# Seventeen zero products in place of thirty-six at the head of a fused attention and feed-forward kernel, with a new order

## The chip, the cores and the metric

The kernel runs on one core of a Trainium2 chip. The metric is the device time of one execution in microseconds (us). The time of the kernel before is the median of three runs. A profile of one more execution was taken by the hardware profiler.

## The reference

A sequence of 2048 rows of 576 values (bf16) passes one block: layer norm, attention with 32 heads of 18 values in four segments of 512 rows, with a memory carried from segment to segment, output projection and residual, then layer norm and a two-layer feed-forward part of width 4608 with gelu, and a second residual.

```python
q, k, v = x @ wq, x @ wk, x @ wv          # split in H=32 heads, N=4 segments
phi = lambda t: jnp.where(t > 0, t + 1.0, jnp.exp(t))
for s in range(N):
    p = _softmax(einsum('bhqd,bhkd->bhqk', qs, ks) * scale + mask)
    a_dot = einsum('bhqk,bhkd->bhqd', p, vs)
    a_mem = einsum(phi(qs), M) / (einsum(phi(qs), z) + 1e-06)
    o = g * a_mem + (1.0 - g) * a_dot      # g = sigmoid(beta), one for each head
    M, z = M + einsum(phi(ks), vs), z + sum(phi(ks))
...
h = x + o_all @ wo                         # attention was given layernorm(x)
h2 = h + (gelu(layernorm(h) @ w1 + b1) @ w2 + b2)
```

## The kernel before, in words

The rows are handled in eight chunks (c) of 256, each of two tiles (t) of 128 rows. A chunk passes projection (`project`), attention (`attend`, with `memory_of` for the memory part), output projection and second layer norm (`output`), `first_layer` (width 4608 in 36 blocks of 128) and `second_layer`. While one chunk is in attention, another is in its feed-forward part.

**Five queues, one list.** The kernel first defines all its steps as operations (`op`, `dma`): each has a name, an engine, the function that issues its instructions, and, for some, a second engine that can do the same work. The operations have running numbers. A list of numbers, `ORDER`, written out by hand into the file, then issues them; what one engine gets, it works off in that order. PE is TensorE (matrix products and transposes), DVE is VectorE, ACT is ScalarE, POOL is GpSimd; SP issues all DMAs.

- `PLACE` gives the PSUM bank of each accumulator. Four banks (0 to 3) are fixed; four more (4 to 7) serve either as single banks or, all four together, as the target of one group of score products (L623). A bank can be written again when its last reader is done.
- `FLIP` holds the operations that go to their second engine.
- `WHOLE` concerns the depth of 576 = 4 x 128 + 64. The last 64 rows of two products can be multiplied side by side in the two halves of the array (`tail`, lines 443 and 750), ahead of their four full products (line 350). For the pairs in `WHOLE`, each product has a full-height last product instead (line 354), with zeros or copies of rows in the other half.

**The head.** At the start PE has nothing to do until the first tile of x is loaded, normalized (statistics L365 and L366, subtraction L379, a copy of the last 64 columns L396, all on DVE), transposed by PE (L409, with an identity that POOL builds) and copied to SBUF (`PTcx`, L412 on DVE or L413 on ACT). Then the first projections run, which also need the weights: `wqkvr` (last 144 columns of wq or wk), `wqkv` (first 432 columns, or all of wv) and `wqkvt` (the last 64 rows, in parts). For the first two tiles the projection is cut into ch 4 (last columns of q and k), ch 1 (k), ch 0 (q), ch 5 and ch 3 (v). To fill the time, PE multiplies zeros:

```python
    for z in range(ZEROS):
        w = warm[min(z, 3)]
        n = 512 if z < 4 else Q
        op(("zeros", z), "PE", lambda w=w, n=n: nc.tensor.matmul(out=bank(w)[:, 0:n], lhsT=pq[:, 0, :], rhs=flat[:, 0:n], start=True, stop=True),
           ["pq"], [w])
```

That is four products of 512 columns and the rest of 256 (Q), on the buffer `pq` that DVE cleared (L333 in the profile). No result of theirs is read. In the order before, 19 stand ahead of the transpose of tile 0 and 17 between it and the transpose of tile 1; then come ch 4 of tiles 0 and 1, ch 1 of both, the transposes of k of tile 0 (`PTk`, L531), ch 0 of both, and so on. Meanwhile ACT, DVE and POOL clear paddings (L259, L292, L308), and `g_exp` (L336, ACT) takes the exponential of beta for the gates.

**DMAs.** SP has in the order before: x tile 0, `wqkvr` of wq, x tile 1, a tail of wk, x tile 2, `wqkvr` of wk, a tail of wq, a tail of wk (54 KB), the main part of wk, beta, the main part of wq, a tail of wv, x tile 3, wv, b1, and then wo, w1 and w2 in parts among the x tiles that follow. Some transposes are DMAs too (`Tx`, `Tk`, `Tq`, `Th`).

**Later steps that are named.** In `first_layer` a bias addition (`F1e`) moves each accumulator to SBUF, on DVE (L771) or, if flipped, ACT (L769); ACT then applies gelu (L792). In attention ACT takes the exponential of a group of 16 score products (L627), POOL masks (L631), PE multiplies with v (L639). `second_layer` is L852. `res` (L686) adds the residual; `MZ` (L561) sums the memory.

Of the kernel before, what the change touches and what calls it, by code (L numbers as in the profile page):

```python
# [16 lines left out]
def kernel(  # L17
# [43 lines left out]
    ZEROS = 36  # L61
# [4 lines left out]
    def sbuf(name, shape, dt=BF16):  # L66
# [29 lines left out]
    }  # L96
    FLIP = {
# [7 lines left out]
    }  # L105
    WHOLE = {
        265, 398, 408, 418, 425, 488, 489, 562, 871, 872, 1104, 1105, 1520, 2160, 2161,
# [221 lines left out]
    warm = [Tok(b) for b in range(4)]  # L329
    for z in range(ZEROS):  # L330
        w = warm[min(z, 3)]
# [547 lines left out]
    for c in range(NCH):  # L879
# [193 lines left out]
```

## Time and profile before

| What | us |
|---|---|
| timed runs | 454.94, 456.51, 457.49 |
| median | 456.51 |
| profiled execution, its own time | 454.46 |
| its span, first to last instruction | 452.4 |
| PE busy | 446.7 |
| ACT busy | 336.1 |
| DVE busy | 267.0 |
| POOL busy | 230.1 |

The span is the profiled part; 2.1 us of the execution lie outside of it. Rows of a timeline have start, length, engine, line of the kernel, instruction, and the tiles written and read; neighbouring instructions of one kind are merged (x19), and brackets tell the idle time ahead of the row and what ended it. Matrix products overlap, so that the length of a single one is more than the distance between two starts.

### The profile page before, as it was taken

The page shows a single profiled execution, that of the slowest core. Times are in us where ns is not written, and L with a number is a line of the kernel's source. Part 1 is how long each engine was busy: PE and PEld are TensorE (multiplying, and loading weights), DVE is VectorE, ACT ScalarE, POOL GpSimd, SP SyncE. Part 2 cuts the span into 40 slices and gives each one's busy share as a digit, 9 for nine tenths or more (in the row PEclk, how much of TensorE's full clock was granted, in tenths as well). Part 3 has the DMA queues.
Part 4 walks back from the last instruction along what each step waited for, and adds up shares of the span by engine and source line. Part 5 has one row for each costly group of instructions (what it writes and reads, how often), then busy time and mean ns, then how long its engine had stood idle before and what let it go on. Part 6 is the DMA issues. An engine that isn't in the chain of part 4 may idle for free.

```text
span 452.4 us, 14531 instructions
## 1 busy us (share of the span) xinstructions
PE 446.7 (99%) x6109; PEld 334.5 (74%) x6109; DVE 267.0 (59%) x612; ACT 336.1 (74%) x327; POOL 230.1 (51%) x414
## 2 busy tenths in 40 slices
PE   8999999999999999999999999999999999999997
PEld 5656887676776777776777667777777888888886
DVE  6989999776868667766665967554432441122311
ACT  7999899988889878879889778797954652634430
POOL 5789775788784678562756775654103302000000
PEclk9999999999999999999999999999999999999999
DMA  6998599945699638698855956785664575655211
GB/s 183 233 251 259 143 207 277 218 103 136 143 183 237 178 101 223 155 173 199 179 159 128 213 143 153 217 232 167 202 185 126 158 195 159 168 178 165 95 54 52
DMA packets 114353, 78.40 MB, mean 173 GB/s; under 512 B 48832, under 2 KB 112240, under 8 KB 114288
## 3 DMA queue, kind: packets, MB, share of 16 engines
q1 hardware_dynamic: 114288, 77.48, 67.4%
q8 instruction: 47, 0.77, 0.7%
q14 instruction: 18, 0.15, 0.1%
HBM read 60.09 MB, written 7.08 MB: 148 GB/s over the span
## 4 chain that ended last, share of the span: by engine, by line
PE 98%; DVE 1%; ACT 0%; issue 0%
PE bank L350 30%; PE bank L852 25%; PE st L350 10%; PE st L852 7%; PE st L623 6%; PE bank L639 5%; PE bank L750 3%; PE bank L683 3%; PE bank L354 2%; PE bank L333 2%; PE st L683 1%; PE bank L593 1%; PE st L750 1%; PE bank L531 1%; PE bank L561 1%; PE bank L443 1%
## 5 line engine op out<-in xcount | busy, mean ns | idle before, releaser
L627 ACT ACTIVATE pt<-st 128x2048 bf16<-128x2048 f32 x80 | 150.1, 1876 | 40.2 <-PE st L623 34.5
L852 PEld LDWEIGHTS <-hT 128*128 128x128 bf16 x1188 | 112.3, 98 | 26.8 <-issue 0.2
L852 PE MATMUL bank<-w_sb,hT 128*128 128x288 bf16 x900 | 127.4, 286 | 0.0
L350 PEld LDWEIGHTS <-w1g 128*128 128x128 bf16 x944 | 86.4, 98 | 19.1 <-issue 7.1
L631 POOL TENSOR_SCALAR_AFFINE_SELECT pt<-pt 128x512 bf16<-128x512 bf16 x128 | 80.6, 645 | 36.7 <-ACT pt L627 36.3
L350 PE MATMUL bank<-xn2T,w1g 128*128 128x256 bf16 (+1 forms) x776 | 96.5, 269 | 0.0
L771 DVE TENSOR_TENSOR hT<-bank,b1T 128x512 bf16<-128x512 f32 x78 | 52.6, 684 | 57.9 <-PE bank L350 56.6
L792 ACT ACTIVATE hT<-hT 128x1536 bf16<-128x1536 bf16 (+4 forms) x25 | 65.9, 2658 | 1.7 <-DVE hT L771 1.4
L769 ACT ACTIVATE hT<-bank,b1T 128x256 bf16<-128x256 f32 x66 | 27.4, 473 | 18.2 <-PE bank L350 18.0
L350 PE MATMUL bank<-wqkv,xT 128*128 128x432 bf16 (+2 forms) x188 | 39.5, 340 | 0.0
L350 PEld LDWEIGHTS <-xT 128*128 128x128 bf16 x264 | 23.7, 98 | 18.5 <-issue 2.4
L852 PE MATMUL st<-w_sb,hT 128*128 128x288 bf16 (+1 forms) x288 | 35.5, 271 | 0.0
L654 DVE STREAM_TRANSPOSE bank<-bank 128x512 f32<-128x512 f32 x32 | 23.2, 725 | 18.4 <-PE bank L639 11.9
L769 ACT ACTIVATE hT<-st,b1T 128x256 bf16<-128x256 f32 x28 | 11.7, 471 | 29.8 <-PE st L350 28.8
L588 POOL TENSOR_TENSOR pq<-ek,pq 128x512 bf16<-128x512 bf16 x24 | 27.8, 1159 | 10.8 <-DVE ek L587 10.4
L623 PE MATMUL st<-QT,KT 32*128 32x128 bf16 x1280 | 32.2, 217 | 0.8 <-DVE hT L771 0.8
L623 PEld LDWEIGHTS <-KT 32*128 32x128 bf16 x1280 | 18.6, 92 | 16.9 <-issue 14.0
L858 DVE TENSOR_TENSOR ot<-bank,hc 128x288 bf16<-128x288 f32 x25 | 11.3, 451 | 28.2 <-PE bank L852 23.5
L586 POOL TENSOR_SCALAR pq<-QT 128x512 bf16<-128x512 bf16 x24 | 14.8, 615 | 19.9 <-PE bank L593 12.0
L639 PE MATMUL bank<-pt,v_aug 128*19 128x128 bf16 x1280 | 24.0, 220 | 0.0
L691 POOL TENSOR_TENSOR h_t<-h_t,b_bc 128x576 f32<-128x576 f32 x16 | 20.4, 1278 | 6.2 <-ACT xn L714 4.3
L771 DVE TENSOR_TENSOR hT<-st,b1T 128x512 bf16<-128x512 f32 x19 | 12.7, 681 | 17.0 <-PE st L350 17.0
(160 smaller groups left out, 663.4 us busy)
## 6 DMA issues: line engine op xcount, KB each, us to landing
w1g<-in_B_w_dram SPq DMA_DIRECT2D x57, 512.0 KB, 4.1
w_sb<-in_B_w_dram SPq DMA_DIRECT2D x12, 432.0 KB, 5.2
wqkv<-in_B_w_dram SPq DMA_DIRECT2D x10, 512.0 KB, 4.4
hd<-h_t SPq DMA_DIRECT2D x16, 288.0 KB, 3.4
hc<-hd SPq DMA_DIRECT2D x32, 144.0 KB, 2.5
w1g<-in_B_w_dram SPq DMA_DIRECT2D x114, 32.0 KB, 3.5
x_b<-in_A_x_dram SPq DMA_DIRECT2D x18, 144.0 KB, 3.5
hT<-in_B_w_dram SPq DMA_DIRECT2D x5, 512.0 KB, 5.0
```

The costliest lines, as they stand in the source:

```text
L350: nc.tensor.matmul(out=acc, lhsT=lhsT_of(slice(0, P), k), rhs=rhs_of(slice(0, P), k), start=start and k == 0, stop=False, skip_group_check ...
L588: op(("m_add", n), "POOL", lambda: nc.gpsimd.tensor_tensor(out=pq[:], in0=e_g, in1=pq[:], op=ALU.add), ["ek"], ["pq"])
L623: nc.tensor.matmul(out=st4[:, i, n * P:(n + 1) * P], lhsT=KTs[(2 * s0 + kt) % NK][rows, g, :], rhs=QTs[(2 * c + qt) % NQ][rows, g, :], sta ...
L627: op(("exp", v), "ACT", lambda pt=pt: nc.scalar.activation(out=pt[:], in_=open_four("scores")[:], func=ACT.Exp, scale=scale), [st], [("pt" ...
L631: op(("mask", v), "POOL", lambda n=n, pt=pt: nc.gpsimd.affine_select(out=pt[:, :, n * P:(n + 1) * P], in_=pt[:, :, n * P:(n + 1) * P], pat ...
L639: nc.tensor.matmul(out=bank(ox)[32 * i:32 * i + E, (g % 4) * P:(g % 4) * P + P], lhsT=v_augs[(2 * s0 + kt) % NV][:, G * i + g, :], rhs=pt[ ...
L654: op(("f_T", n), "DVE", lambda: nc.vector.transpose(out=bank(ox), in_=bank(ox)), [], [ox])
L691: op(("hb", t), "POOL", lambda: nc.gpsimd.tensor_tensor(out=h_t[:], in0=h_t[:], in1=b2_bc[:], op=ALU.add), ["b2"], hk)
L769: nc.scalar.activation(out=dst[:, j, :], in_=acc()[:, j, :], func=ACT.Identity, bias=b1T[:, j0 + j:j0 + j + 1], scale=1.0)
L771: op(name, "DVE", lambda: nc.vector.tensor_tensor(out=dst, in0=acc(), in1=bias, op=ALU.add), [tok, "b1T"], keys, alt=("ACT", by_act), afte ...
L792: op(("gelu", c, f0, f), "ACT", lambda: nc.scalar.activation(out=hT[:, f0:f, :], in_=hT[:, f0:f, :], func=ACT.Gelu_apprx_tanh), [], [("hT" ...
L852: nc.tensor.matmul(out=bank(b)[:, 0:w], lhsT=hT[:, q, tl * P:(tl + 1) * P], rhs=w2_sb[:, q, hs], start=(q == 0), stop=(q == NF - 1))
```

## The change

`ZEROS` is 17 instead of 36. `PLACE`, `FLIP`, `WHOLE` and `ORDER` hold other values throughout. Numbers of operations behind the zeros are lower by 19, so the lists must be read by names; what follows was read that way.

- Zero products: 11 ahead of the transpose of tile 0, 4 ahead of that of tile 1, 2 behind it. Then ch 4 of tiles 0 and 1, ch 1 of both, `PTk` of tile 0, ch 0 of both, as before; the transpose of tile 2 (`PTx`) comes two places earlier than before, ahead of ch 5.
- SP: x tile 0, `wqkvr` of wk, x tile 1, x tile 2, beta, a tail of wq, `wqkvr` of wq, a tail of wk, the main part of wk, the 54 KB tail of wk, the main part of wq, x tile 3, a tail of wv, wv, a tail of wv, x tiles 4 and 5, two chunks of w1 (512 KB each), a part of wo, b1, the DMA transpose of tile 3.
- ACT: ten clears, with `g_exp` in eighth place among them, ahead of the copy of xT of tile 0 (before: eleven clears, `g_exp` behind the copies of both tiles). The copy of xT of tile 1 goes from ACT to DVE.
- DVE: ahead of the first statistics stand the clears of `pq` and of `MZacc`, the constant `mhalf`, one padding, and one clear of weights (before: eight clears).
- POOL: six clears, then the identity (before: the identity first).
- Banks: ch 4 and ch 1 of a tile share a bank (3 for tile 0, 4 for tile 1); before they had one each.
- `WHOLE`: 13 pairs instead of 15. Other bank for 278 of 363 accumulators. `FLIP` has 130 entries instead of 134.

```diff
-    ZEROS = 36
+    ZEROS = 17
...
     PLACE = {
-        0: 0, 1: 1, 2: 2, 3: 3, 4: 1, 5: 4, 6: 5, 7: 5, 8: 3, 9: 1, 10: 2, 11: 5, 12: 3, 13: 4, 14: 4, 15: 6, 16: 4,
...
+        0: 0, 1: 1, 2: 2, 3: 3, 4: 2, 5: 2, 6: 5, 7: 3, 8: 3, 9: 0, 10: 1, 11: 2, 12: 3, 13: 4, 14: 6, 15: 4, 16: 4,
...
     FLIP = {
-        15, 24, 26, 28, 33, 39, 44, 48, 49, 50, 51, 57, 60, 61, 66, 151, 153, 155, 157, 161, 173, 175, 177, 179, 181,
...
+        15, 28, 29, 31, 32, 33, 34, 35, 36, 43, 45, 49, 50, 51, 53, 57, 62, 63, 64, 65, 66, 132, 134, 136, 138, 142,
...
     WHOLE = {
-        265, 398, 408, 418, 425, 488, 489, 562, 871, 872, 1104, 1105, 1520, 2160, 2161,
+        246, 399, 406, 469, 470, 543, 647, 774, 852, 853, 1501, 2141, 2142,
     }
...
     ORDER = [
-        23, 57, 41, 0, 22, 26, 28, 32, 29, 67, 55, 3, 58, 30, 1, 68, 15, 43, 59, 46, 144, 24, 56, 45, 69, 70, 71, 145,
...
+        23, 57, 24, 42, 54, 25, 0, 29, 58, 30, 26, 28, 59, 27, 38, 125, 67, 68, 126, 69, 70, 71, 6, 22, 127, 1, 72,
...
```

333 rows, old and new, of tables (FLIP, ORDER, PLACE) are left out of this document.

## The prediction

> **What bounds the kernel now.** I read the page's busy shares first, then what the tensor engine (PE) waited for, then the stages, then the head instruction by instruction.
>
> ```profile
> span 452.4 us, 14531 instructions
> PE 446.7 (99%) x6109; PEld 334.5 (74%) x6109; DVE 267.0 (59%) x612; ACT 336.1 (74%) x327; POOL 230.1 (51%) x414
> ```
>
> PE is busy in 446.7 of 452.4 us, so only three things can move the time: what PE does, where it stands idle, and work that it does for nothing. The view of waits for PE says where it is idle:
>
> ```profile
> PE bank L333 <- DVE pq L292: 1.2, 1, 1.2
> PE st L623 <- DVE hT L771: 0.8, 1, 0.8
> PE bank L561 <- DVE h_t L686: 0.6, 1, 0.6
> PE st L350 <- ACT xT L413: 0.2, 1, 0.2
> ```
>
> That is 1.2 us ahead of the first zero product and 1.6 us in three later waits. The stages show where the two long ones can arise:
>
> ```profile
> 16.00:46.00 30.00, 29.56 (x486) 17.76 (x486) 27.40 (x65) 28.02 (x28) 25.94 (x52) 1.00 0.95 237
> 75.00:430.00 355.00, 355.00 (x4749) 266.42 (x4747) 197.66 (x445) 265.20 (x253) 176.62 (x298) 1.00 0.67 171
> ```
>
> The columns after the length are PE, PEld, DVE, ACT and POOL. From 75 to 430 us PE has no gap at all. From 16 to 46 us DVE is at 27.40 and ACT at 28.02 of 30.00: there the three engines are nearly level, and a late helper stops PE. The remaining work for nothing lies in the head:
>
> ```profile
> 1.24 5.05 PE L333 MATMUL bank<-pq 128*128 128x512 bf16 x19 [1.24 <-DVE pq L292]
> 2.65 0.58 POOL L259 MEMSET wqkv<- 64x576 bf16 x1
> 3.77 0.82 DVE L365 BATCH_NORM_STATS2 stats_p<-x_p 128x6 f32<-128x288 bf16 x2
> 5.14 0.59 SPq L273 DMA_DIRECT2D wqkv<-in_A_wk_dram  x1
> 5.27 0.18 DVE L396 COPY xn<-xn 128x64 bf16<-128x64 bf16 x1
> 5.77 0.50 SPq L281 DMA_DIRECT2D beta_bc<-in_A_beta_dram  x1
> 6.12 0.45 PE L409 MATMUL st<-ident,xn 128*128 128x128 bf16 x5
> 6.32 0.43 SPq L273 DMA_DIRECT2D wqkv<-in_A_wq_dram  x1
> 6.41 2.02 PE L333 MATMUL bank<-pq 128*128 128x256 bf16 x17
> 6.86 0.18 DVE L396 COPY xn<-xn 128x64 bf16<-128x64 bf16 x1
> 6.96 0.68 ACT L413 COPY xT<-st 128x640 bf16<-128x640 bf16 x1
> 7.99 0.43 SPq L273 DMA_DIRECT2D wqkv<-in_A_wv_dram  x1
> 8.27 0.44 PE L409 MATMUL st<-ident,xn 128*128 128x128 bf16 x5
> 8.55 0.65 PE L350 MATMUL bank<-wqkv,xT 128*128 128x288 bf16 x4
> 10.12 0.89 PE L350 MATMUL st<-wqkv,xT 128*128 128x432 bf16 x4
> 10.27 0.23 ACT L336 ACTIVATE g_bc<-beta_bc 128x32 f32<-128x32 bf16 x1 [0.83 <-DMA beta_bc<-in_A_beta_dram]
> 12.39 0.89 PE L350 MATMUL st<-wqkv,xT 128*128 128x432 bf16 x4
> 15.56 0.41 PE L350 MATMUL bank<-wqkv,xT 128*128 128x144 bf16 x4
> ```
>
> Rows are start, length, engine, line. The normalized first tile is complete at 5.27 + 0.18 = 5.45, yet its transpose starts at 6.12, behind 19 zero products. The second tile is complete at 7.04, its transpose starts at 8.27, behind 17 more. So the filler, and not data, sets the first projection at 8.55. The first 19 stream 4 x 512 + 15 x 256 = 5888 columns in 5.05 us, 0.86 ns a column; the other 17 stream 4352 in 2.02 us, 0.46 ns. PE ran at half rate at first and at full rate from about 6 us on. This has to be read from the rows.
>
> How soon the projections could follow the loads comes from the view of DMAs cut to the first 12 us (size, issue to landing):
>
> ```profile
> wqkv<-in_A_wv_dram SPq DMA_DIRECT2D x1, 576.0 KB, 6.3
> x_p<-in_A_x_dram SPq DMA_DIRECT2D x3, 144.0 KB, 2.3
> wqkv<-in_A_wk_dram SPq DMA_DIRECT2D x1, 432.0 KB, 3.7
> wqkv<-in_A_wq_dram SPq DMA_DIRECT2D x1, 432.0 KB, 5.3
> beta_bc<-in_A_beta_dram SPq DMA_DIRECT2D x1, 8.0 KB, 4.5
> ```
>
> Added to the issue times: wk's main part lands at 5.14 + 3.7 = 8.84 and is first used at 10.12; wq's at 6.32 + 5.3 = 11.62, used at 12.39; wv at 7.99 + 6.3 = 14.29, used at 15.56. PE is 1.28, 0.77 and 1.27 us late against them.
>
> **The change, part by part.**
>
> *Zero products, 36 to 17.* The new order has 11 ahead of the first transpose, 4 between the two and 2 behind. Eleven are 4 x 512 + 7 x 256 = 3840 columns; at 0.86 ns that is 3.3 us, so they end at 1.24 + 3.3 = 4.5. What else the first transpose needs: DVE's queue now has five short items ahead of the first statistics and leaves a clear of the weights, a ones column, one padding and the wo clear for later, so that the statistics can follow x's landing, not before 0.79 (SP's first issue, unmoved) + 2.3 = 3.1, against 3.77. That is 0.7 earlier at most; below nothing it can't go, as DVE has no new work there. Tile 0 is then complete at 5.45 - 0.7 = 4.75 and tile 1 at 6.34. POOL builds the identity behind six clears now; at the longest clear's 0.58 each from 0.8 us it is done by about 4.8 as well, a bound from above. So the first transpose runs at 4.8, four zeros and the second follow to 6.9, two more zeros to 7.3.
>
> *The first projection* then waits for ACT's copy of xT. ACT had 11 clears ahead of it (copy at 6.96) and now has 10 and the exponential of beta. Taken unchanged, the copy ends at 6.96 + 0.68 = 7.64: 0.9 us ahead of 8.55. If the exponential is late it is later; see the rivals.
>
> *The loads.* The main part of wk is ninth in both orders, wq's eleventh, wv's fourteenth; beta moves from tenth to fifth, and a 54 KB tail of wk from eighth to tenth, behind the main part. So the bulk lands as before, and the second projection (ch 1) now waits for a tail that comes just behind 8.84: I take 9.2, with 8.84 and 9.4 as bounds (one issue step of 0.6 us). It also shares its PSUM bank with the first one, whose eviction must be out; that chain of 7.64 + 0.65 + an eviction ends ahead of 9.2. Gain here 10.12 - 9.2 = 0.9. The next lot waits for wq: 12.39 - 11.62 = 0.77 is the most that can be kept. Behind it wv allows 1.27, which doesn't bind. **The head gains 0.8 us** (bounds: 0, if something late takes it, and 1.1 if wq lands 0.3 sooner without the tail ahead).
>
> *Products of the body.* For two operations of layer tails, WHOLE chooses between two half-height products side by side and a full-height last product each. The entries go from 15 to 13: one projection pair and one pair of layer one less. Array switches between tilings, counted in the two order lists, go from 268 to 273. The prices:
>
> ```profile
> 10.85 0.35 PE L354 MATMUL st<-wqkv,xT 128*128 128x432 bf16 x1
> 11.03 0.89 PE L350 MATMUL st<-wqkv,xT 128*128 128x432 bf16 x4
> 18.84 0.36 PE L443 MATMUL bank<-wqkv,xT 64*128 64x432 bf16 x2
> 19.13 0.42 PE L350 MATMUL bank<-wqkv,xT 128*128 128x144 bf16 x4
> 92.65 2.13 PE L852 MATMUL bank<-w_sb,hT 128*128 128x288 bf16 x16
> 94.71 0.40 PE L623 MATMUL st<-QT,KT 32*128 32x128 bf16 x16
> 436.25 9.31 PE bank L852 x76
> ```
>
> Start to start a last product is 11.03 - 10.85 = 0.18, two are 0.36; the half-height pair is 0.29 with a switch behind it. Sixteen products that end in a switch take 94.71 - 92.65 = 2.06, against 16 x 9.31 / 76 = 1.96: a switch is 0.10. So a pair alone is 0.19, one WHOLE less saves 0.36 - 0.19 = 0.17 for a projection, about as much (0.2, an estimate from the columns) for layer one, together 0.4; five switches cost 0.5. Net +0.1 us. All other products are the same ones, in another order.
>
> *Order, banks, engines of the body.* 278 of 363 bank choices and most of the order differ; DVE's operations rise from 603 to 615, ACT's fall from 253 to 246, POOL's from 377 to 372. From 75 us on PE had no gap with DVE at 197.66 of 355.00, so twelve operations are hidden there. Between 16 and 75 us they are not free. The two waits, 0.8 and 0.6, may vanish (-1.4) or come more often (+0.8 each). Without a row that favours one I take the same two again: 0.
>
> *Sum.* The profiled execution took 454.46 us, its span 452.4 and 2.1 around it. 454.46 - 0.8 + 0.1 = 453.8. The median of the timed runs is 456.51, so 2.05 above that execution. One thing that can differ between executions is where the half rate ends: if the 17 later zeros run at 0.86 instead of 0.46 ns, they take 4352 x 0.40 = 1.7 us more, all on the path. The new order has two behind the second transpose: 512 x 0.40 = 0.2. I carry 0.2 instead of 2.05: **454.0 us**, 2.5 below the median. Had it the whole 2.05 again, it would be 455.8.
>
> The Trainium skill (TensorE: Matmul & The Clock Gate, Part 1) says that the array starts at half clock and is released after about one busy window of 3.4 us, with free-running windows. The trace agrees in kind: half rate for about 5 us from 1.24. The same page (Why this matters for your kernels) asks for at least 4 us of unbroken work, which speaks against 11 zeros and a gap; by it the sum would be that of the second rival.
>
> **The rivals.**
>
> 1. *The two later waits vanish too*, because helpers stand better in the order: 454.0 - 1.4 = 452.6. For it: PE has slack nowhere else. Against: DVE has more to do, not less.
>
> 2. *The half rate lasts into the projections.* The new head has PE idle near 4.5 to 4.8 and again from 7.3 to 7.64, and what gaps the release tolerates no row shows, since the old head has none. Work from 7.64 on at half rate costs half its time. If the full rate comes 3.4 to 7 us later than 7.64, that is 1.7 to 3.5; the head's 0.8 is more than gone: 454.0 + 2.6 = 456.6, no difference from 456.51.
>
> 3. *The head's gain is given back.* ACT's queue is in order, and the exponential of beta stands ahead of the xT copy. Beta took 4.5 us; issued fifth, some four steps of 0.6 ahead of 5.14, it would land at 7.2, and the exponential, two clears and the copy end near 9.2, later than 8.55. Or PE comes 0.8 earlier to 16 us and waits there for DVE. Either way 454.0 + 0.8 + 0.5 = 455.3.
>
> 4. *Slower: DVE decides between 16 and 75 us.* Score products need all four shared banks empty, so one late bias addition (L771) on DVE stops PE for 0.8 us, as once now. The old order fits one real course of loads, with two such waits; a new one, with 12 more DVE operations, may not. By the order list about twenty score groups lie in the stretch. Six more waits cost 4.8: 458.8; eight, 460.4. It decides from six on.
>
> That the filler is not on the path at all, so nothing changes, is contained in 3.
>
> **How the numbers follow.** About 0.5% (2.3 us) is what a measurement of this kernel can tell from no change: under 454.2 is faster, over 458.8 slower. The forecast case has 0.44, spread over about 453.2 to 455.2 by its bounds, 0.30 of it on the faster side; rival 1 has 0.18, all faster; rival 2 0.08 and rival 3 0.10, nearly all the same; rival 4 0.20, taken as slower. Together 0.48 faster, 0.32 same, 0.20 slower. The range leaves a tenth at each end: 451.9 below, where the two waits vanish and wq lands sooner; 459.2 above, within rival 4.
>
> **What would show it.** Right: first projection near 7.6, wk's at 9.2, wq's at 11.6; PE's waits together under 2 us behind 16 us; PE's busy time lower by about 2 us, as filler is gone; DVE still near nine tenths between 16 and 46 us. Rival 2 would show products of 432 columns 0.36 us apart instead of 0.18 behind 8 us; rival 3 ACT waiting for beta ahead of the xT copy; rival 4 several rows of waits of scores for L771. The prediction is wrong if PE's busy time falls while its waits in the body grow by more, or if the head starts its first projection after 8.5.

## The result and the profile after

The changed kernel takes 452.21 us (median of six, 452.07 to 453.55), the kernel before 455.52 (median of six, 454.41 to 457.49). The ratio is 0.9929, with a 95% interval of 0.9904 to 0.9955: faster by 0.7%, 1.8 us below the forecast of 454.0 and inside its range. The profiled execution takes 452.16 us, against 454.46.

The page's span and busy shares of the changed kernel:

```profile
span 450.3 us, 14470 instructions
PE 445.4 (99%) x6090; PEld 331.0 (74%) x6090; DVE 271.4 (60%) x624; ACT 331.1 (74%) x318; POOL 230.2 (51%) x409
```

PE has nineteen instructions less and 1.3 us less work; the other 0.8 of the span's 2.1 us is less idle time. The view of waits, PE's rows, all of them:

```profile
PE bank L333 <- DVE pq L292: 1.2, 1, 1.2
PE bank L350 <- DMA wqkv<-in_A_wk_dram: 0.6, 1, 0.6
PE bank L350 <- ACT xT L413: 0.2, 1, 0.2
```

The waits for L771 (0.8) and in L561 (0.6) are gone, and a new one of 0.6 for wk stands in the head. The view by stages says the same (columns: length, then PE, PEld, DVE, ACT, POOL with their counts, the granted clock, DMA share, GB/s); the stage from 46 to 75 us of the kernel before, not shown so far, comes first, by itself:

```profile
46.00:75.00 29.00, 28.03 (x571) 23.89 (x570) 26.85 (x57) 26.20 (x19) 18.42 (x36) 1.00 0.85 206
```

```profile
16.00:46.00 30.00, 30.00 (x515) 18.32 (x513) 27.78 (x65) 27.63 (x28) 25.34 (x53) 1.00 0.88 203
46.00:75.00 29.00, 29.00 (x564) 24.23 (x562) 26.79 (x58) 27.46 (x19) 21.68 (x40) 1.00 0.99 210
75.00:430.00 355.00, 354.93 (x4728) 265.36 (x4726) 201.18 (x455) 258.58 (x244) 172.35 (x286) 1.00 0.68 173
```

Before, PE was idle for 0.44 + 0.97 = 1.41 us between 16 and 75 us; after, for nothing, although DVE is as full (27.78 of 30.00, and 26.79 of 29.00). The two waits that are gone stand, in the timeline of the kernel before, at the very end of the first of these stages and at the end of the second:

```profile
46.13 0.46 PE L561 MATMUL bank<-v_aug,phik_pad 128*128 128x76 bf16 x8 [0.57 <-DVE h_t L686]
71.94 0.40 PE L623 MATMUL st<-QT,KT 32*128 32x128 bf16 x16 [0.84 <-DVE hT L771]
```

The head, from the timeline of the changed kernel (start, length, engine, line):

```profile
1.24 3.38 PE L333 MATMUL bank<-pq 128*128 128x512 bf16 x11 [1.24 <-DVE pq L292]
2.73 0.43 SPq L281 DMA_DIRECT2D beta_bc<-in_A_beta_dram  x1
4.61 0.71 PE L409 MATMUL bank<-ident,xn 128*128 128x128 bf16 x5
5.12 1.06 PE L333 MATMUL bank<-pq 128*128 128x256 bf16 x4
5.47 0.23 ACT L336 ACTIVATE g_bc<-beta_bc 128x32 f32<-128x32 bf16 x1
6.20 0.53 PE L409 MATMUL st<-ident,xn 128*128 128x128 bf16 x5
6.42 0.68 ACT L413 COPY xT<-bank 128x640 bf16<-128x640 bf16 x1
7.16 0.67 PE L350 MATMUL bank<-wqkv,xT 128*128 128x288 bf16 x4 [0.21 <-ACT xT L413]
9.15 0.90 PE L350 MATMUL bank<-wqkv,xT 128*128 128x432 bf16 x4 [0.55 <-DMA wqkv<-in_A_wk_dram]
11.44 0.89 PE L350 MATMUL st<-wqkv,xT 128*128 128x432 bf16 x4
14.43 0.41 PE L350 MATMUL bank<-wqkv,xT 128*128 128x144 bf16 x4
```

The first projection stands at 7.16 instead of 8.55, 1.39 us earlier. Not all of it lasts: 0.55 goes into the wait for wk, and wq's lot starts at 11.44 instead of 12.39, a gain of 0.95; ch 5 at 14.43 instead of 15.56. So the 2.1 us of the span are 0.95 of the head and 1.41 of waits in the body, less about 0.3 that went back in small pieces (0.07 of it is idle time behind 75 us). (In ACT's queue the exponential of beta stands ninth, behind eight of the ten clears, and not eighth.)

### The profile page after: what moved, and what is told of

Read it like the earlier page. It is cut to its first block, busy times and chain, and to the rows that moved or that the text cites. A ratio compares the mean times of both kernels' runs of the same rounds, so it can differ in the third digit from the quotient of the medians.

```text
span 450.3 us, 14470 instructions
## 1 busy us (share of the span) xinstructions
PE 445.4 (99%) x6090; PEld 331.0 (74%) x6090; DVE 271.4 (60%) x624; ACT 331.1 (74%) x318; POOL 230.2 (51%) x409
## 4 chain that ended last, share of the span: by engine, by line
PE 96%; DMA 2%; SPq 1%; issue 0%; DVE 0%
PE bank L350 30%; PE bank L852 25%; PE st L350 10%; PE st L852 6%; PE st L623 6%; PE bank L639 5%; PE bank L683 3%; PE bank L750 3%; PE bank L354 2%; PE st L683 1%; PE st L750 1%; DMA w1g<-in_B_w_dram 1%; PE bank L593 1%; PE bank L531 1%; DMA wqkv<-in_A_wk_dram 1%; PE bank L561 1%
## 5 line engine op out<-in xcount | busy, mean ns | idle before, releaser
L852 PE MATMUL bank<-w_sb,hT 128*128 128x288 bf16 (+1 forms) x936 | 130.2, 284 | 0.0
L350 PE MATMUL bank<-xn2T,w1g 128*128 128x256 bf16 (+1 forms) x728 | 89.6, 268 | 0.0
L771 DVE TENSOR_TENSOR hT<-bank,b1T 128x512 bf16<-128x512 f32 x74 | 50.1, 681 | 37.9 <-PE bank L350 36.6
L769 ACT ACTIVATE hT<-bank,b1T 128x256 bf16<-128x256 f32 x70 | 28.9, 474 | 31.9 <-PE bank L350 31.8
L858 DVE TENSOR_TENSOR ot<-bank,hc 128x288 bf16<-128x288 f32 (+1 forms) x26 | 11.7, 448 | 41.9 <-PE bank L852 38.2
L852 PE MATMUL st<-w_sb,hT 128*128 128x288 bf16 (+1 forms) x252 | 33.0, 277 | 0.0
L771 DVE TENSOR_TENSOR hT<-st,b1T 128x512 bf16<-128x512 f32 x25 | 16.7, 681 | 23.1 <-PE st L350 23.1
L350 PE MATMUL st<-xn2T,w1g 128*128 128x256 bf16 x216 | 29.4, 273 | 0.0
L657 POOL TENSOR_TENSOR r<-r,omg 128x16 f32<-128x16 f32 x32 | 7.0, 219 | 36.9 <-DVE r L655 34.6
L769 ACT ACTIVATE hT<-st,b1T 128x256 bf16<-128x256 f32 x20 | 8.1, 472 | 21.3 <-PE st L350 21.3
```

The lines of the kernel that those rows point to most:

```text
L350: nc.tensor.matmul(out=acc, lhsT=lhsT_of(slice(0, P), k), rhs=rhs_of(slice(0, P), k), start=start and k == 0, stop=False, skip_group_check ...
L769: nc.scalar.activation(out=dst[:, j, :], in_=acc()[:, j, :], func=ACT.Identity, bias=b1T[:, j0 + j:j0 + j + 1], scale=1.0)
L771: op(name, "DVE", lambda: nc.vector.tensor_tensor(out=dst, in0=acc(), in1=bias, op=ALU.add), [tok, "b1T"], keys, alt=("ACT", by_act), afte ...
L852: nc.tensor.matmul(out=bank(b)[:, 0:w], lhsT=hT[:, q, tl * P:(tl + 1) * P], rhs=w2_sb[:, q, hs], start=(q == 0), stop=(q == NF - 1))
```

## The experiments

"Old" is the order of the kernel before, "new" the changed one; "zeros 11/4/2" are those ahead of the first transpose, between the two, and behind them. The ratio is to the kernel before, run on the same chip in turn (its medians there: 456.36, 455.91 and 455.82 us for experiments 1 to 4, 5 to 8, 9 to 12). The last two columns come from the profile of each: the start of wq's lot, and PE's idle time between 16 and 75 us by the view of stages. From 75 to 430 us PE is idle for 0.25 us or less, but for 0.55 in number 2, 0.60 in 4, 0.84 in 8, 0.82 in 12, and 0.83 in number 3, whose wait for L771 ends only at 75.88.

| Kernel | median us (n) | ratio, 95% | wq's lot | idle 16-75 |
|---|---|---|---|---|
| before | 455.52 (6) | 1 | 12.39 | 1.41 |
| after | 452.21 (6) | 0.9929 (0.9904-0.9955) | 11.44 | 0.00 |
| 1 old, 17 zeros | 456.17 (12) | 0.9998 (0.998-1.0017) | 12.41 | 2.45 |
| 2 new, 36 zeros | 453.36 (7) | 0.9942 (0.9922-0.9962) | 11.98 | 0.00 |
| 3 new head, old rest | 458.37 (12) | 1.0041 (1.002-1.0062) | 11.55 | 3.38 |
| 4 old head, new rest | 453.60 (6) | 0.9949 (0.9929-0.9969) | 12.09 | 0.34 |
| 5 old, two DVE moves | 454.69 (12) | 0.9987 (0.9974-1.0) | 12.69 | 0.63 |
| 6 old, DMA transpose earlier | 455.85 (12) | 1.0011 (0.9995-1.0028) | 12.77 | 1.49 |
| 7 new, 4 zeros | 454.34 (12) | 0.9977 (0.9957-0.9996) | 12.67 | 0.31 |
| 8 new, wk one load earlier | 455.53 (12) | 1.0006 (0.999-1.0022) | 11.46 | 0.21 |
| 9 old, beta early | 456.03 (12) | 0.9997 (0.9982-1.0013) | 12.93 | 1.86 |
| 10 as 9, 17 zeros | 455.61 (12) | 0.9998 (0.9982-1.0014) | 12.28 | 2.26 |
| 11 as 10, two DVE moves | 454.82 (12) | 0.9985 (0.9969-1.0001) | 11.74 | 1.87 |
| 12 new, beta late | 457.99 (9) | 1.0053 (1.0036-1.0071) | 16.69 | 0.20 |

### 1. The old order with 17 zeros

```diff
-ZEROS = 36      zeros 19/17/0, old ORDER
+ZEROS = 17      zeros 11/4/2, old ORDER otherwise
```

> The old order with 17 zero products, placed as in the new one: 11, 4 and 2. All else is the old kernel. If the filler sets the old head: both tiles are ready at 5.45 and 7.04 and the copy of xT ends at 7.64, so the first projection starts near 7.65 (8.55 before), wk's at 8.9 to 9.0 (10.12), wq's near 11.65, when wq has landed (12.39). Span 452.4 - 0.75 = 451.6. If the spread of the old runs comes from zeros at half rate, the timed runs also lie within 1 us of each other, median near 453.7. Rival: the loads or DVE take all of it back by 75 us: span 452.4, median as the old one.

No gain: ratio 0.9998. The rows of the timeline that explain it:

```profile
7.69 0.44 PE L409 MATMUL st<-ident,xn 128*128 128x128 bf16 x5 [1.06 <-ACT xT L413]
10.16 0.23 ACT L336 ACTIVATE g_bc<-beta_bc 128x32 f32<-128x32 bf16 x1 [1.31 <-DMA beta_bc<-in_A_beta_dram]
11.74 0.62 PE L531 MATMUL bank<-ident,qk_pad 128*128 128x128 bf16 x8 [0.22 <-ACT qk_pad L504]
12.41 0.89 PE L350 MATMUL st<-wqkv,xT 128*128 128x432 bf16 x4
```

The filler hid other holds. In the old `PLACE` the transposes of tiles 0 and 1 share a bank, so the second waits until ACT has copied the first out: 7.69 instead of a ready tile at 7. And ACT stands 1.31 us at the exponential of beta, so that `qk_pad` behind it comes late and PE waits in L531. wq's lot starts at 12.41, as with 36 zeros (12.39). By then a third hold has come up. The load of wq was issued at 6.33, as before, and the view of DMAs has for it:

```profile
wqkv<-in_A_wq_dram SPq DMA_DIRECT2D x1, 432.0 KB, 6.0
```

It landed at 6.33 + 6.0 = 12.33, against 11.62 before, less than 0.1 us ahead of its use. So this execution does not tell what the bank and beta cost by themselves: the load alone would have held wq's lot. The rows of 32 to 37 us show one more hold:

```profile
29.84 2.27 SPq L154 DMA_TRANSPOSE xT<-xn  x1
33.17 0.29 PE L623 MATMUL st<-QT,KT 32*128 32x128 bf16 x8 [0.41 <-DMA KT<-hT]
36.69 0.36 PE L443 MATMUL bank<-wqkv,xT 64*128 64x432 bf16 x2 [0.65 <-DVE r L655]
```

The view of DMAs around that issue gives its time to landing:

```profile
xT<-xn SPq DMA_TRANSPOSE x1, 6.8
```

29.84 + 6.8 = 36.64: the tile that L443 reads landed 0.05 us ahead of its start. L655 is named as what came last, but it ended at 36.41 + 0.25 = 36.66; the two fall together here. In the kernel before, where the order at this place is the same, L443 starts at 35.23 and L655 only at 35.67, so L443 doesn't need it. Number 10 shows the landing as the releaser.

### 2. The new order with 36 zeros

```diff
-ZEROS = 17      zeros 11/4/2, new ORDER
+ZEROS = 36      zeros 19/17/0, new ORDER otherwise
```

> The new order with 36 zero products, placed as in the old one: 19 ahead of the transpose of tile 0, 17 between it and that of tile 1. If filler is on the path: first projection near 8.5 (7.16 new), wq's near 12.7 (11.44), span 450.3 + 1.2 = 451.5, and a wider spread of the timed runs, by up to 1.7 us. Rival (the filler only fills waits for loads): wq's projection within 0.3 us of 11.44, span 450.3 to 450.6.

0.9942 against 0.9929: most of the gain stays with all 36 zeros. The first projection starts at 8.13, wk's lot at 9.70, wq's at 11.98, 0.54 later than with 17. The span is 451.5 as expected, but only 0.54 of the 1.2 us is the head; another 0.48 is idle time behind 75 us. The medians differ by 1.15 us, the ratios by 0.0013 (0.6 us), and their intervals overlap. The ratio is the fairer of the two, since the kernel before differs by 0.84 us between the two sets of runs: the filler alone is worth about 0.5 us, at most 1.

### 3 and 4. The head of one, the rest of the other

```diff
-ORDER, PLACE, FLIP, WHOLE of one kernel throughout
+3: of the new one up to the fifth score group (about 25 us), then of the old
+4: of the old one up to the second value group (about 25 us, 36 zeros), then of the new
```

> Order, banks and engines of the new kernel up to the fifth group of score products (about 25 us), of the old kernel from there on. If the gain has two parts that add: the waits of the sums of the memory (L561, 0.6) and of the scores for L771 (0.8) come back behind 45 us, and the span is 450.3 + 1.2 = 451.5; the old spread of about 3 us comes back if it arises in the body. Rival (all of the gain is the head's): span 450.3. Rival (the waits were caused by the old head): no wait over 0.3 behind 45 us.

> The old kernel up to the second group of value products (about 25 us), with 36 zeros; the new one from there on. If the parts add: the head costs 1.0 again, the body has no wait over 0.3: span 450.3 + 1.0 = 451.3. If the spread arises in the body, the timed runs lie within 1.5 us of each other as those of the new kernel do; if it is the zeros at half rate, they spread by 3 us as those of the old one.

Number 4, with the old head, keeps 0.9949; number 3, with the new head, is slower than before by 0.4%. So the larger part of the gain lies behind 25 us. The six runs of number 4 lie within 1.35 us of each other, with all 36 zeros, by its expectation a sign that the spread of the kernel before arises in the rest. Number 3 has its cause in its own seam: loads that the new head had left for later come, at the seam, ahead of the DMA transpose of k of tile 2. Its waits, that row, and the products behind the wait:

```profile
PE st L623 <- DMA KT<-hT: 2.2, 1, 2.2
PE bank L561 <- DVE h_t L686: 0.9, 1, 0.9
PE st L623 <- DVE hT L771: 0.8, 1, 0.8
```

```profile
29.03 1.24 SPq L154 DMA_TRANSPOSE KT<-hT  x1
34.80 1.62 PE L350 MATMUL bank<-wqkv,xT 128*128 128x432 bf16 x4
```

It is issued at 29.03, against 27.10 before and 25.45 after, and PE waits 2.2 us for it. Behind that wait PE comes back at half rate: four products of 432 columns take 1.62 instead of the 0.90 of four like them at 29.76, and the granted clock is 0.81 from 32 to 36 us and 0.76 from 36 to 40. That is about 1.7 us more (0.19 + 0.24 of 4 us). Seven of the twelve timed runs have a granted clock of 0.996 over the whole and take 458.35 to 460.31 us, the other five 455.77 to 457.59. The last two waits are those of the kernel before, unmended. So number 3 doesn't price the new head; it shows only that a rest which doesn't follow on from the head's SP queue can lose more than the head gains.

### 5. Two moves on DVE in the old order

```diff
-DVE: ..., g_gmz, res(1,1), ..., F1qe(0,0), ...
+DVE: ..., res(1,1), ..., F1qe(0,0), g_gmz, ...
-DVE: F1e(0,11), F1e(0,10), F1e(0,12)
+DVE: F1e(0,10), F1e(0,12), F1e(0,11)
```

> The old kernel with two moves in DVE's queue alone: one copy for the gates (L344) from directly ahead of a residual addition (L686) to six places behind it, and one bias addition (L771, of an accumulator in a fixed bank) behind the next two, which hold shared banks that a group of scores waits for. If these two waits are the old body's own, in any course of the loads: both fall from 0.7 and 0.9 to under 0.4, span and median lower by 1.2 (median near 455.2 where the old one has 456.4), the spread of about 3 us unchanged. Rival (DVE's total work is the limit there, the waits turn up elsewhere): median within 0.4 of the old one.

The wait for L771 shrinks to 0.2 and the one of L561 for L686 is gone; a later L561 waits 0.2 for L771. By the view of waits:

```profile
PE st L623 <- DVE hT L771: 0.2, 1, 0.2
PE bank L561 <- DVE hT L771: 0.2, 1, 0.2
```

Together the waits lose 1.0 us. The median is 1.2 lower than that of the runs beside it; the ratio, 0.9987, touches 1 with its interval. The moves are worth something between nothing and 1.2 us, which isn't the gain of the new order.

### 6. The DMA transpose of k of tile 2, three places up in the old order

```diff
-SP: Tx 4, x_b 0, wo 3, x_b 1, Tk 2
+SP: Tx 4, Tk 2, x_b 0, wo 3, x_b 1
```

> The old kernel with one move in SP's queue alone: the DMA transpose of k of tile 2 goes ahead of three loads (two of x, one of wo), as soon as the transpose of tile 4. If the spread of the old runs comes from this transpose landing too late for the scores that need it (2.2 us of waiting in the run with the new head): issue about 2 us earlier, no wait of scores for it in the profile, the upper half of the timed runs comes down, median near 455.4, spread under 2.5. Rival (the spread has another source): median and spread as the old ones, 456.4 and 3.6.

1.0011: no effect, though the transpose is issued 1.98 us earlier (25.12) and no wait for it shows; the runs still spread over 3.95 us. The wait on KT that numbers 1 and 3 show is not what the kernel before loses by itself.

### 7. The new order with four zeros

```diff
-ZEROS = 17      zeros 11/4/2
+ZEROS = 4       zeros 4/0/0 (512 columns each)
```

> The new kernel with the first four zero products alone (512 columns each), none behind them; PE then stands idle from 3.0 to 4.6 and again at 5.2 and from 6.7 to 7.1. If the clock rises by the time since the first product: full rate near 6.4 as before, first projection at 7.15, span 450.3 within 0.3. If it asks for dense work: half rate until 10 to 14, first projections of 432 columns 0.36 apart, wk's lot ends 1.5 to 1.8 later, span 451.5 to 453.

PE then stands idle twice ahead of the transposes, and stays at half rate. Timeline:

```profile
4.66 0.72 PE L409 MATMUL bank<-ident,xn 128*128 128x128 bf16 x5 [1.53 <-DVE xn L379]
6.25 0.71 PE L409 MATMUL st<-ident,xn 128*128 128x128 bf16 x5 [0.87 <-DVE xn L379]
7.13 1.14 PE L350 MATMUL bank<-wqkv,xT 128*128 128x288 bf16 x4 [0.16 <-ACT xT L413]
9.50 1.65 PE L350 MATMUL bank<-wqkv,xT 128*128 128x432 bf16 x4
12.67 0.89 PE L350 MATMUL st<-wqkv,xT 128*128 128x432 bf16 x4
```

The first projection is as early as after (7.13), but four products of 432 columns take 1.65 at 9.50 and 0.89 at 12.67: half rate until about 11.3. wq's lot comes 1.23 later than after, the span is 1.6 longer, the median 2.1. The remaining zeros carry the clock: what they cost is nothing, since tile 0 isn't ready earlier, and what they bring is this.

### 8. wk one load earlier in the new order

```diff
-SP: x_p 1, x_p 2, beta, ..., wqkvt 1 (54 KB)
+SP: x_p 1, beta, ..., wqkvt 1 (54 KB), x_p 2
-DVE: bnp 2, bnp 2, aggrp 2, PTcx 1
+DVE: PTcx 1, bnp 2, bnp 2, aggrp 2
```

> The new kernel with the load of x tile 2 moved behind wk's last tail (so that wk comes one place, about 0.5 us, earlier), and on DVE the statistics of tile 2 behind the copy of xT of tile 1. The wait of 0.6 for wk at 9.15 is the largest left behind the first product. If the loads are limited by their order: wk's projection at 8.6 to 8.8, wq's at 11.0 to 11.2, span 449.9, a little faster than the new kernel. Rival (bandwidth: wq still lands at 11.0 and the sum of the loads sets ch 5): less than 0.2 gained.

wk's lot starts at 8.67, 0.48 earlier, and nothing is left of it: wq's lot waits 0.4 for its own load and starts at 11.46, and DVE stands idle 1.92 us for x tile 2, so that a copy of k behind it in its queue (L534) comes at 14.82 instead of 12.93 and holds PE's transpose of tile 2 for 1.2 us. ch 5 stands at 15.79 instead of 14.43, 0.84 us of idle time follow behind 75 us, and the ratio is 1.0006. The wait of 0.55 for wk in the changed kernel is balanced against the next load.

### 9 to 11. Beta early, then 17 zeros, then the DVE moves, in the old order

```diff
 9: SP   -beta behind the main part of wk     +beta behind x tile 2 (sixth)
10: as 9, zeros 11/4/2, and the transpose of tile 0 in bank 2 instead of 4
11: as 10, and the DVE moves of 5
```

> The old kernel with the load of beta moved from tenth to sixth place in SP's queue, right behind x tile 2. In the old runs ACT stands idle 0.4 to 1.7 us for beta, with the evictions of the first projections queued behind. If that is the old head's limit beside the filler: beta lands near 5.5, no wait of ACT for it, the spread of wq's projection (12.09 to 12.77 in the runs so far) shrinks, but its time stays near 12.4, as 36 zeros still hold the first projection: median 0 to 0.4 lower. Rival (beta is hidden in any case): no difference.

> The kernel of the run before with 17 zeros as well (11, 4, 2) and the transpose of tile 0 in bank 2 instead of the one that the transpose of tile 1 uses. If filler, beta and the shared bank together hold the old head: first projection near 7.6, wk's near 8.95, wq's at 11.6 (12.4 with 17 zeros alone); median 0.8 below the old one's. Rival (the old body gives it back, as with the new head in front of the old rest): median not below the old one's.

> The same with the two moves on DVE that took 1.2 us. If the parts add up: no wait over 0.4 behind 16 us in the profile, median 0.8 + 1.2 = 2.0 below the old one's, about 60% of the new kernel's gain. Rival (the moves on DVE fit only the old head's course): less than 1.2 below.

With beta early ACT no longer waits for it, but the filler still holds the head: 0.9997. Number 10 is rid of the filler, the shared bank and the wait for beta together: its first projection stands at 7.69, wk's lot at 10.02, wq's at 12.28, 0.65 ahead of number 9, but only 0.11 ahead of the profile of the kernel before. wk's lot waits 0.65 for its load, which beta has pushed back one place (it lands at 5.62 + 4.3 = 9.92, against 5.16 + 4.2 = 9.36 in number 1). The ratio is 0.9998; its interval reaches down to 0.9982, so that a gain of up to 0.8 us is not excluded. What PE waits for instead is in its waits and in rows of 26 to 37 us:

```profile
PE st L623 <- DVE hT L771: 0.7, 1, 0.7
PE bank L561 <- DVE h_t L686: 0.6, 1, 0.6
PE st L623 <- DMA KT<-hT: 0.3, 1, 0.3
```

```profile
26.75 2.42 SPq L154 DMA_TRANSPOSE KT<-hT  x1
29.90 1.96 SPq L154 DMA_TRANSPOSE xT<-xn  x1
36.50 0.36 PE L443 MATMUL bank<-wqkv,xT 64*128 64x432 bf16 x2 [0.71 <-DMA xT<-xn]
```

The view of DMAs has 6.6 us from that issue to landing, 36.5: PE starts L443 in the same moment, and L655 had ended 0.08 earlier. In the kernel before the rows are these, with 5.8 to landing:

```profile
29.29 1.22 SPq L154 DMA_TRANSPOSE xT<-xn  x1
35.23 0.36 PE L443 MATMUL bank<-wqkv,xT 64*128 64x432 bf16 x2
```

29.29 + 5.8 = 35.09, 0.14 us ahead of use: the old order had little room there. In number 5 the two stand at 35.68 and 35.74, in number 6 at 35.73 and 35.76. A PE that came earlier would wait for it.

But number 10 loses more than that: with the earlier head L443 starts 1.27 us later than in the kernel before, as the transpose of x is issued 0.61 later and takes 0.8 longer to land. Ahead of it the issue of the transpose of k takes 2.42 us instead of 1.24 (27.10 before), and 2.70 and 2.79 in numbers 1 and 11, the two other kernels of the old order with 17 zeros. What makes it longer, no run isolates. In the changed kernel the transpose of x is issued at 28.82, takes 5.3 and is used at 34.38, 0.26 later.

Number 11 has the head of number 10, but wk's lot does not wait this time and wq's stands at 11.74. It takes the L771 and L561 waits down as number 5 did (three of 0.2 are left), and its ratio is close to number 5's: 0.9985. PE waits again in L443 (0.66) and for KT (0.45). Head and moves don't add up: the 2.0 us expected would be a ratio of 0.9956, below the interval.

### 12. Beta late in the new order

```diff
-SP: x_p 1, x_p 2, beta, ..., wqkvt 1 (54 KB)
+SP: x_p 1, x_p 2, ..., wqkvt 1 (54 KB), beta
```

> The new kernel with beta in tenth place in SP's queue, as in the old one, behind wk's last tail. ACT's queue is in order, with the exponential of beta ahead of the copy of xT: beta lands near 9.5 to 10.2, the copy ends near 11.3, first projection at 11.3 instead of 7.16, and PE idle from about 7 on. By then wk, wq are there, so the projections run without a wait: wq's at 15, ch 5 at 17.6 instead of 14.4: 3 us and more, median near 455.5. Rival (the copy overtakes, or beta is quick): within 0.5 of the new kernel.

Timeline of ACT and PE:

```profile
10.04 0.23 ACT L336 ACTIVATE g_bc<-beta_bc 128x32 f32<-128x32 bf16 x1 [4.50 <-DMA beta_bc<-in_A_beta_dram]
10.99 0.68 ACT L413 COPY xT<-bank 128x640 bf16<-128x640 bf16 x1
11.72 1.14 PE L350 MATMUL bank<-wqkv,xT 128*128 128x288 bf16 x4 [4.90 <-ACT xT L413]
14.10 1.21 PE L350 MATMUL bank<-wqkv,xT 128*128 128x432 bf16 x4
15.33 0.89 PE L350 MATMUL st<-wqkv,xT 128*128 128x432 bf16 x4
```

An 8 KB load five places later costs 5.8 us of the median. ACT works its queue off in order: the copy of xT stands behind the exponential, PE is idle for 4.90 us, and comes back at half rate (1.14 instead of 0.67 for four products of 288 columns) until about 15. In the new order of ACT the place of beta decides over more than the whole gain; in the old order (number 9) it made no difference that shows.

## Why the prediction was right, and where not

**The head, 0.8 forecast, 0.95 measured.** First projection 7.6 forecast, 7.16 measured: ACT's copy ran at 6.42, not at the old 6.96, behind ten clears instead of eleven, and beta, which had landed by 5.47, did not hold it. wk's lot 9.2 forecast, 9.15 measured, but this is luck: the tail that the forecast had PE wait for landed at 5.62 + 3.7 = 9.32, when the lot was under way, and what held the lot was the main part, at 4.99 + 4.1 = 9.09 instead of 8.84. wq's 11.62 forecast, 11.44 measured, as wq landed at 6.18 + 4.8 = 10.98 and no longer bound. The bounds (0 to 1.1) hold it.

**That the filler sets the head.** Only half right. The step stopped at the first hold found: number 1 took the filler away and wq's lot stayed at 12.41. Behind the filler stood a shared bank and ACT's wait for beta, and in that execution wq's own load, at 12.33 where the sum had 11.62. Without the bank and beta, wk's load was the next (number 10). The prediction priced the filler and the loads at their lengths before; the bank that the two transposes shared it did not see. A load of wq took 4.5 to 6.0 us to land in these profiles (numbers 11 and 1), so that a gain of 0.8 in the head is within what one load can take.

**The body's waits, 0 forecast, 1.41 measured.** This is the term that was mis-sized: the case called rival 1 came true beside the forecast case. The prediction looked for both waits between 16 and 46 us; the rows have them at 45.6 to 46.1 and at 71.1 to 71.9. "Against: DVE has more to do" was no argument: DVE has 27.78 of 30.00 us in the first stage after and 27.40 before, 26.79 and 26.85 of 29.00 in the second, and number 5 shows that the order within its queue is enough: two moves took the waits from 1.4 to 0.4. Which moves of the new order do it was not tried. Every kernel with the old rest has 0.63 to 3.38 us idle between 16 and 75 us, every one with the new rest 0 to 0.34.

**The products, +0.1.** PE's busy time was to fall by about 2 and fell by 1.3 us. The rows of zeros make 5.05 + 2.02 = 7.07 before and 3.38 + 1.06 + 0.38 = 4.82 after, 2.25 less. Of the 0.95 that came back, 0.35 are the two transposes, which ran at half rate in part (0.71 + 0.53 against 0.45 + 0.44). The other 0.6 is the most that switches and other products can have cost; the sum of the span leaves them 0.2 to 0.3.

**The carry, 0.2 of 2.05.** The size came out, by luck: the median after stands 0.05 above its profiled execution, but the reason given covers a part at most. With 36 zeros the first projection started at 8.55, 8.13, 8.24, 8.85, 8.17 and 9.09 in six profiles (before and numbers 2, 4, 5, 6, 9), a spread of 1.0 us by where the half rate ends; in the new head with 17 zeros at 7.16, 7.13 and 7.13 (after, 3, 8). So fewer zeros do take spread away from the head, but 1.0 and not 1.7. The timed runs go with the rest instead: number 1, with 17 zeros and the old rest, spreads over 2.89 us (12 runs) and keeps its median at 456.17; number 4, with 36 zeros and the new rest, over 1.35 (6 runs), the changed kernel over 1.48 (6 runs). With so few runs that is a sign and no proof. Another part is that the profile of before was a favourable execution: later runs of that kernel lie between 454.06 and 458.09, and 454.46 is near the lower end. With the six runs of the result its median is 455.52, 1.06 above it and not 2.05.

**The sum.** Of the 1.8 us between 454.0 and 452.2, the body's waits are 1.4, the head and the carry 0.15 each, and 0.2 lies outside of the span (452.16 - 450.3 = 1.86, against 2.06); the products took some 0.15 back.

**Rival 2, half rate into the projections.** Not in the changed kernel: the four zeros at 5.12 take 1.06 us, the two at 6.57 0.38, so that the full rate came near 6.4. It is a true price: numbers 7 and 12 show it. How little was enough is best seen in number 10, where the transpose behind 3.24 us of zeros and a gap of 0.80 us ran at full rate:

```profile
1.25 3.24 PE L333 MATMUL bank<-pq 128*128 128x512 bf16 x11 [1.25 <-DVE pq L292]
5.29 0.45 PE L409 MATMUL bank<-ident,xn 128*128 128x128 bf16 x5 [0.80 <-DVE xn L379]
```

The Trainium skill (TensorE: Matmul & The Clock Gate, Why this matters for your kernels) asks for at least 4 us of unbroken products; number 10 needed less. Four zeros with gaps of 1.53 and 0.87 (number 7) were too few. The same section's warning that an idle time of some 3 us brings the slow clock back agrees with number 12, at 4.90. Number 3 came back at half rate after 2.16 us already (2.2 in its waits), so here the measurement is the stricter.

**Rival 3, the gain given back.** Wrong for the new order: beta was estimated to land at 7.2, and it had by 5.47. In the old order ACT's wait for beta stood there all along (0.83 in the row quoted before), and an earlier head (numbers 1 and 10) met the landing of the DMA transposes. The rival looked for the taker on DVE; in the old rest it was SP's queue.

**Rival 4, DVE decides.** Not seen: no wait for L771 in any kernel with the new rest. Number 3 came to the slower side, through a DMA transpose.

**What stays open.** Which moves of the new rest remove the waits wasn't isolated, neither for L561 and L771 nor for those of 32 to 37 us: number 6 moved one of the two transposes, and the one of x wasn't moved by itself. Why its landing takes 4.0 to 6.8 us in kernels with different heads isn't known. Nor is the source of the spread of the kernel before: none of its runs has a granted clock under 0.999, so it isn't a loss of the clock as in number 3.

## What to carry to other kernels

Filler in front of a chain can stand beside other holds of the same length: follow each engine's queue in order (a bank shared, a small load ahead of a copy) before the filler is priced, since taking away one of them can move nothing. A head that comes earlier is worth something only if the next transfers have room; look for the landing that ends within a tenth of a microsecond of its use. On an engine that is 99% busy, two waits of half a microsecond behind the changed stage can be the larger part of what a change brings, and a stage where three engines are nearly level has to be priced for the better as well as for the worse.

## What the chip showed that was not expected

- The end of the half rate differs between executions of nearly the same head. The transpose of tile 0 was already at full rate at 4.56 in number 12 (0.45 us), still at half rate at 6.12 in number 9 (0.74), with products running from 1.24 in both:

```profile
4.56 0.45 PE L409 MATMUL bank<-ident,xn 128*128 128x128 bf16 x5
```

```profile
6.12 0.74 PE L409 MATMUL st<-ident,xn 128*128 128x128 bf16 x5
```

The Trainium skill (TensorE: Matmul & The Clock Gate, Part 1) speaks of windows that run freely, so that the point depends on where the first product falls; the two rows agree in kind, though the 1.5 us between them is more than the half microsecond of variation that the page gives.

- The issue of the same DMA transpose of a 128-row tile of x takes 1.2 us on SP, or up to 2.3 (1.22 before, 1.96 in number 10, 2.27 in number 1). Issue to landing is 4.0 to 6.0 us where the issue is short (numbers 8 and 5), and 6.6 and 6.8 in numbers 10 and 1.
- One kind of DVE copy, of 32 x 144 values, took 0.22 to 1.46 us in the kernel before. The median of its four instances, between 18 and 53 us, is 0.60; what stretches it was not tried.
